# Selection matmuls for the last 16 spectrum rows, and batch 1's first stage inside the first MLP steps

## The chip, the cores and the metric

One core of a Trainium2 chip. The metric is device time of that core in microseconds (us), the median of several executions. "Step" means one of the 400 MLP steps into which the kernel's plan is cut (50 token groups of 8 steps); steps 0 to 47 belong to batch 0.

## The reference, cut to what matters

```python
# x (8, 3136, 256), filt_r and filt_i (1569, 256), U (3136, 32), V (32, 3136)
X = np.fft.rfft(x, axis=1)                       # over the 3136 tokens
y = np.fft.irfft(X * (filt_r + 1j * filt_i), n=3136, axis=1)
h = y.transpose(0, 2, 1) @ U @ V                 # low-rank token mixing
u = y + h.transpose(0, 2, 1)
out = u + np.maximum(u @ w_ch1, 0.0) @ w_ch2     # channel MLP, 256 -> 1024 -> 256
```

## The kernel before

The two transforms are matmuls over 3136 = 64 x 49, each in two stages. Stage 1 writes its result to DRAM (`ct1`) and reads it back in another order (`a`); stage 2, the filter multiply and stage 3 give the spectrum after the filter, which goes through DRAM again (`ct2`, read back as `e`); stage 4 gives `ut`, the input of the MLP. Batch 0 skips the first trip by transposing on TensorE. An eviction is the copy of a result out of TensorE's accumulators (0.59 us for 128x512 on ScalarE, line 273). Batches 1 to 7 run their stages between the MLP steps of the batch ahead, by a plan:

```python
def load_x(b, c, after=None):             # POOL issues the loads of x
    ...                                   # c == 3: the last 64 rows
        t = sb.tile([128, 4, XW], F16, tag="x", bufs=4, name="x")
        if after is not None:             # a copy that waits for `after`
            nc.gpsimd.tensor_copy(t[0:1, 0, 0:1], after[0:1, 0:1])
        for h in range(2):
            nc.gpsimd.dma_start(t[h:128:2, :, 0:2 * DM], ...)

def st1(b):                               # stage 1: 12 pieces and a last one
    for c in range(3):
        ...                               # 8 matmuls, 4 evictions into asb
        for h in range(2):                # the sync engine issues the stores
            nc.sync.dma_start(dram(ct1[b], ...), asb[64 * h:64 * h + 64])
        ...
    nc.scalar.copy(al, pf[0:64, 0:DM])    # the last piece
    nc.sync.dma_start(dram(ct1[b], ...), al)

def load_a2(b, k):                        # read-back for stage 2
    t = sb.tile([98, 4 * DM], F16, tag="a2", bufs=4, name="a2")
    nc.sync.dma_start(t, dram(ct1[b], 4 * k * DM, ...))
...
low_rank(0)
for n, _ in enumerate(st1(1)):            # stage 1 of batch 1 in the head
    ...
stage4(groups[0], 0)                      # then the first MLP step
stage4(groups[0], 1)
...
def x_after(b):                           # x of batch 2 waits for relu of step 3
    for c in range(4):
        load_x(b, c, groups[0].h[3] if c == 0 else None)
at(4, x_after, 2)
...
for n, gr in enumerate(groups):
    for t in range(8):
        ...
        mm1(gr, t)                        # first MLP matmul and relu
        if n: mm2_part(groups[n - 1], t)  # second MLP matmul of the group ahead
        for f, a in plan[8 * n + t]:      # what the plan holds for this step
            f(*a)
```

## Time and profile before

| | us |
|---|---|
| median of the runs beside the changed kernel (4) | 555.31 (554.28 to 556.38) |
| profiled run | 555.2 |
| first MLP matmul | 61.2 |
| step 48 begins (batch 0 done) | 134.7 |
| rest | 420.5 |

What the sync engine's queue issued, in order of time (start, us that the issues took, engine, line, operation, target and source, count):

```profile
49.15 0.31 SPq L329 DMA_DIRECT2D ct<-esb  x1
52.45 1.10 SPq L438 DMA_DIRECT2D e<-ct  x2
53.66 5.83 SPq L277 DMA_DIRECT2D ct<-asb  x6
59.59 1.05 SPq L286 DMA_DIRECT2D ct<-al  x1
62.65 1.62 SPq L320 DMA_DIRECT2D a<-ct  x4
```

In this program a read-back is issued only when the stores before it have landed (between 48 and 70 us the trace has the sync engine wait for `ct<-esb` ahead of its reads of `e`, 1.9 us at the longest). So the gap between a store's issue and its read's issue shows how long the store took to land, at most: 3.3 us for batch 0's last spectrum tile (49.15 to 52.45), and 3.1 us for the last piece of batch 1's stage 1 (59.59 to 62.65). Second, POOL after that:

```profile
66.50 0.18 POOL L168 COPY x<-hring 1x1 f16<-1x1 f16 x1 [12.12 <-ACT hring L492]
67.02 4.25 POOL L170 DMA_DIRECT2D x<-in_x_dram  x6 [0.33 <-POOL x L168]
```

POOL stood idle for 12.12 us until a relu of ScalarE (line 492) let it copy one element; only then did it issue the load of batch 2's x. That 1x1 copy is a hold: it keeps 1.5 MB of loads back until stage 1 of batch 1 has been stored and its read-back issued.

### The profile page before, as it was taken

To read this page: it belongs to the slowest core of one execution; us is meant where nothing else is said; L and a number is where in the kernel's file an instruction comes from. 1 tells how busy PE (TensorE), PEld (TensorE's weight loads), DVE (VectorE), ACT (ScalarE), POOL (GpSimd) and SP (SyncE) were. 2 spreads that over 40 slices of the span, in tenths; PEclk is the share of its full clock that TensorE was granted. 3 is DMA by queue.
4 is the path that set the end of the run, shared out by engine and by line. 5 is a ranking of instruction groups with operands and counts; after the bars stand their busy time and mean duration, and the time that the engine had idled before them with its cause. 6 is when DMAs were issued, how large, how long until landed. Compare 5 with 4: busy or idle time off the path is not lost.

```text
span 555.2 us, 11638 instructions
## 1 busy us (share of the span) xinstructions
PE 517.2 (93%) x4491; PEld 375.3 (68%) x4491; DVE 353.1 (64%) x409; ACT 390.8 (70%) x684; POOL 282.4 (51%) x194
## 2 busy tenths in 40 slices
PE   5976689997999999999999999999999999999996
PEld 2634356664767777777776777777786777777775
DVE  6764675755756686758846785858746887643332
ACT  8566868774777688767776788677777577765663
POOL 5778179951883165915683175806563297300000
PEclk9999899997999999999999999999999999999999
DMA  9998876894669468774879468865653553333212
GB/s 194 157 170 192 225 141 187 209 230 130 174 184 250 125 176 199 173 204 137 193 222 221 123 173 228 166 199 152 186 170 121 141 167 121 106 113 115 96 77 87
DMA packets 85432, 92.06 MB, mean 166 GB/s; under 512 B 6741, under 2 KB 69416, under 8 KB 85376
## 3 DMA queue, kind: packets, MB, share of 16 engines
q1 hardware_dynamic: 67968, 75.12, 45.5%
q0 software_dynamic: 16960, 15.91, 19.1%
q8 instruction: 35, 0.57, 0.4%
q10 hardware_dynamic: 448, 0.28, 0.3%
q14 instruction: 21, 0.17, 0.1%
HBM read 57.42 MB, written 49.77 MB: 193 GB/s over the span
## 4 chain that ended last, share of the span: by engine, by line
PE 70%; POOL 10%; DVE 7%; DMA 6%; ACT 4%; issue 2%; DVEq 0%; ACTq 0%; POOLq 0%; SPq 0%
PE psum L521 25%; PE psum L488 24%; PE psum L352 4%; PE psum L344 4%; PE psum L477 4%; PE psum L497 3%; PE psum L266 3%; POOL y L634 3%; DMA x<-in_x_dram 3%; POOL x L170 2%; DVE ut L482 1%; DVE tb L632 1%; PE psum L416 1%; DMA w1sb<-in_moe_w_ch_dram 1%; ACT asb L273 1%
## 5 line engine op out<-in xcount | busy, mean ns | idle before, releaser
L492 ACT ACTIVATE hring<-psum 128x512 f16<-128x512 f32 (+1 forms) x416 | 237.7, 576 | 104.5 <-PE psum L488 103.2
L488 PE MATMUL psum<-ut,w1sb 128*128 128x512 f16 (+1 forms) x832 | 240.3, 370 | 6.4 <-ACT hring L492 3.0
L521 PE MATMUL psum<-w2sb,hring 128*128 128x256 f16 x1536 | 230.9, 273 | 0.0
L634 POOL TENSOR_TENSOR y<-ta,tb 128x1024 f16<-128x1024 f16 x56 | 120.5, 2159 | 159.4 <-DVE tb L632 115.5
L521 PEld LDWEIGHTS <-hring 128*128 128x128 f16 x1536 | 143.3, 98 | 63.8 <-issue 3.8
L482 DVE CAST ut<-psum 128x512 f16<-128x512 f32 x96 | 71.1, 741 | 108.3 <-PE psum L477 88.2
L488 PEld LDWEIGHTS <-w1sb 128*128 128x128 f16 x832 | 104.6, 145 | 27.3 <-issue 10.4
L529 DVE COPY och<-psum 128x512 f32<-128x512 f32 x96 | 66.2, 689 | 47.3 <-PE psum L497 46.6
L326 ACT CAST esb<-psum 98x512 f16<-98x512 f32 x128 | 74.7, 586 | 21.6 <-PE psum L344 16.0
L628 DVE TENSOR_TENSOR ta<-psum,fb 128x1024 f16<-128x1024 f32 x41 | 50.0, 1218 | 7.9 <-PE psum L352 6.9
L273 ACT CAST asb<-psum 128x512 f16<-128x512 f32 x78 | 45.7, 589 | 12.3 <-PE psum L266 11.2
L497 PE MATMUL psum<-idn,ut 128*128 128x128 f16 x392 | 54.0, 220 | 0.0
L477 PEld LDWEIGHTS <-e 96*128 96x128 f16 x768 | 35.9, 99 | 25.5 <-issue 10.2
L630 DVE TENSOR_TENSOR tb<-psum,fc 64x1024 f16<-64x1024 f32 x41 | 50.3, 1226 | 0.9
L632 DVE TENSOR_TENSOR tb<-psum,fc 64x1024 f16<-64x1024 f32 x41 | 49.9, 1218 | 0.8
L477 PE MATMUL psum<-sv,e 96*128 96x64 f16 x768 | 38.8, 194 | 6.5 <-DMA e<-ct 3.7
L344 PE MATMUL psum<-y,g 128*98 128x512 f16 x105 | 39.9, 380 | 3.0 <-POOL y L634 1.5
L497 PEld LDWEIGHTS <-ut 128*128 128x128 f16 x392 | 38.4, 98 | 4.9
L628 POOL TENSOR_TENSOR ta<-pc,fb 128x1024 f16<-128x1024 f16 x15 | 32.4, 2159 | 10.7 <-ACT pc L638 10.7
L352 PE MATMUL psum<-a,w2t 98*128 98x512 f16 x113 | 34.3, 379 | 1.7 <-DVE tb L632 1.6
L266 PE MATMUL psum<-x,wf 128*128 128x256 f16 x168 | 31.3, 274 | 2.8 <-DVE asb L271 1.0
L630 POOL TENSOR_TENSOR tb<-pc,fc 64x1024 f16<-64x1024 f16 x15 | 31.8, 2122 | 1.2
(93 smaller groups left out, 373.6 us busy)
## 6 DMA issues: line engine op xcount, KB each, us to landing
out_dram<-och SPq DMA_DIRECT2D x47, 512.0 KB
ct<-esb SPq DMA_DIRECT2D x64, 196.0 KB
x<-in_x_dram POOLq DMA_DIRECT2D x48, 256.0 KB, 8.1
e<-ct SPq DMA_DIRECT2D x48, 256.0 KB
a<-ct SPq DMA_DIRECT2D x56, 196.0 KB
ct<-asb SPq DMA_DIRECT2D x42, 256.0 KB
wf<-wf SPq DMA_DIRECT2D x3, 256.0 KB
w1sb<-in_moe_w_ch_dram POOLq DMA_DIRECT2D x1, 512.0 KB, 6.8
```

Source lines behind the costliest of these rows:

```text
L326: nc.scalar.copy(esb[b, k][:, 2 * half:2 * half + 2, :].rearrange("p s d -> p (s d)"), pe[0:98])
L344: nc.tensor.matmul(pe[0:98], g3[:, m, :], v, start=(n == 0), stop=(n == len(parts) - 1))
L477: nc.tensor.matmul(pu[:, 64 * i:64 * i + 64], e2[b, c][:, i, 128 * dh:128 * dh + 128], sv[:, 64 * r:64 * r + 64], start=(i == 0), stop=Tru ...
L482: nc.vector.tensor_copy(o, v)
L488: nc.tensor.matmul(ph[:, 0:n], w1sb[:, dh, :, t], gr.ut[:, dh, 0:n], start=(dh == 0), stop=(dh == 1))
L492: nc.scalar.activation(h[:, 0:n], ph[:, 0:n], RELU)
L497: nc.tensor.matmul(o[:, dh * 128:dh * 128 + 128], gr.ut[:, dh, t0:t0 + n], idn, start=False, stop=(dh == 1), skip_group_check=True)
L521: nc.tensor.matmul(o, gr.h[tt][:, i * 128:(i + 1) * 128], w2sb[:, tt, :], start=(tt == 0), stop=False, skip_group_check=True)
L529: nc.vector.tensor_copy(gr.och[:, 2 * y:2 * y + 2, :].rearrange("p j d -> p (j d)"), gr.pc)
L628: eng.tensor_mul(ta, p, va)
L630: eng.tensor_mul(tb[0:64], p[64:128], vb[64:128])
L634: nc.gpsimd.tensor_add(ys[k], ta, tb)
```

## The change

Its intent is to shorten the head, the time before the first MLP step. Four parts matter here:

1. The first token group of batch 0 needs all 64 spectrum rows. 48 are read back from DRAM early; the last 16 are picked out of on-chip tiles by matmuls with 0/1 matrices (`sel`), and the low-rank term H gets its own matmul into the same accumulator.
2. VectorE does all 16 spectrum multiplies of batch 0 (POOL did four).
3. Ten of the thirteen pieces of batch 1's stage 1 go from the head into MLP steps 0 to 4; six of that batch's eight spectrum tiles take a form with twice the TensorE work and less filter preparation.
4. Loads move: w1 behind a copy of V on POOL, w2 behind the first `ut`, and x of batch 2 to steps 4 to 7.

The diff, cut to its core (the whole also halves the stage-1 table's load and trims tiles to 113 partitions):

```diff
 def mid_first():
+        def pick(j):                     # rows 48..63 by selection
+            for i in range(2):
+                sl = 2 * (j - 12) + i
+                for g in range(4):
+                    nc.tensor.matmul(zp[32 * g:32 * g + 32], sel[:, g, 28 - 4 * sl:60 - 4 * sl],
+                                     esb[0, j // 2][:, 2 * (j % 2) + i, :], ...)
 ...
+                if k == 5:
+                    load_e2(0, 0, 48)    # the 48 rows of the first group
 ...
         for c in range(4):
             load_x(1, c)
-        nc.gpsimd.dma_start(w2sb, moe_w_ch2.rearrange("(cc t) e -> cc (t e)", t=8))
+        nc.gpsimd.tensor_copy(sv[64:96, :]..., vnat...)
+        nc.gpsimd.dma_start(w1sb, moe_w_ch1...)
 ...
-            if j in (7, 9, 12, 14): ...  # POOL multiply
+            nc.vector.tensor_mul(uv, pz[0:NZ], fin)
 ...
-    for n, _ in enumerate(st1(1)): ...
+    for k in (4, 5, 0, 1, 2, 3):
+        make_fc(k, nc.gpsimd.tensor_copy)
+    nc.gpsimd.tensor_copy(w2sb[0:1, 0, DM:DM + 1], groups[0].ut[0:1, 0, 0:1])
+    nc.gpsimd.dma_start(w2sb[:, :, 0:DM], ...)
 ...
+            for k, q in ((4, 5), (0, 5), (1, 5), (5, 6), (2, 12), (3, 15), (6, 18), (7, 22)):
+                at(q, fetch, k)          # read-backs of batch 1 at steps 5 ..
+            for k, q, d in ((4, 9, 18), (5, 17, 27)):
+                at(q, two, k)            # first stage 2 at step 9
 ...
-    at(4, x_after, 2)
+    for n in range(5):
+        for _ in range(2):
+            at(n, step1, 1)              # stage 1 of batch 1
+    for c in range(4):
+        at((4, 4, 6, 7)[c], load_x, 2, c)
+        at((33, 38, 43, 45)[c], load_x, 3, c)
 ...
-            plan_st1(b, 12, (0, 1, 3, 4, 5, 7))
+            plan_st1(b, 16, (0, 1, 3, 4, 5, 7))     # b == 2
```

## The prediction

> **What bounds the kernel now.** I read the page's slices first, then busy time in stretches that I chose, then the chain that ended last over the first 62 us, then TensorE in order of time where it is not full. One slice is 555.2/40 = 13.9 us:
>
> ```profile
> PE   5976689997999999999999999999999999999996
> ...
> PEclk9999899997999999999999999999999999999999
> DMA  9998876894669468774879468865653553333212
> ```
>
> TensorE is full from the sixth slice on, with one dent (slice 10, 125 to 139 us, where the clock falls too) and a short tail. So from there only removed TensorE work helps; before it, and in the dent, what helps is an earlier end of a wait. The stretches give sizes (61.2 us is the first MLP matmul, line 488; counting its pairs in order of time, the 48 MLP steps of batch 0's six groups end at 134.68 us):
>
> ```profile
> core 0: us, PE busy (x) PEld busy (x) DVE busy (x) ACT busy (x) POOL busy (x), PEclk, DMA share, GB/s
> 0.00:61.20 61.20, 44.95 (x312) 26.55 (x313) 36.77 (x45) 41.14 (x47) 39.91 (x50) 0.94 0.99 186
> ...
> 61.20:134.68 73.48, 60.69 (x503) 42.27 (x500) 50.03 (x61) 50.50 (x87) 47.28 (x33) 0.96 0.77 181
> 134.68:555.20 420.52, 411.55 (x3684) 306.51 (x3682) 266.27 (x304) 299.12 (x550) 195.23 (x111) 1.00 0.58 160
> ```
>
> Three terms, then: a head of 61.2 us, batch 0's MLP of 73.5 us in which TensorE is idle 73.48 - 60.69 = 12.8 us, and a rest of 420.5 us that is TensorE-bound (411.55 busy). The head's chain ends so:
>
> ```profile
> 45.26 2.13 POOL uv L397
> ...
> 48.69 1.08 PE psum L416 x32
> ...
> 53.82 0.88 PE psum L266 x6
> ...
> 57.03 2.72 PE psum L234 x6
> ...
> 60.21 0.74 DVE ut L482
> ```
>
> The last of 16 spectrum multiplies waits for POOL (2.13 us against 1.17 to 1.22 us on VectorE). Then come the low-rank product, stage 1 of batch 1 (line 266, 50.2 to 56.6), warming matmuls (line 234), and the first group's stage 4, which also needs the spectrum written to DRAM and read back. From the last spectrum row (about 48.6) to the first MLP matmul are 12.6 us. The dent:
>
> ```profile
> 125.76 0.61 PE L488 MATMUL psum<-ut,w1sb 128*128 128x512 f16 x2
> 130.09 0.58 PE L477 MATMUL psum<-sv,e 96*128 96x64 f16 x8 [3.73 <-DMA e<-ct]
> ...
> 131.32 1.06 PE L488 MATMUL psum<-ut,w1sb 128*128 128x512 f16 x2
> ```
>
> Batch 1's spectrum came back from DRAM too late by 3.7 us, and the same pair of matmuls afterwards takes 1.06 instead of 0.61 us.
>
> [...] the idle 3.73 us are followed by 1.04 to 1.06 us pairs until 135.5, so the dent costs more than its wait. [...] 32 low-rank matmuls of 256 columns span 1.08 us, some 34 ns each, against 109 ns start to start for the full-width ones (four of line 521 begin in about 0.437 us). The new selection matmuls have that form. [...]
>
> **The change, part by part.** *Start.* The table for stage 1 is loaded at half size and doubled by two VectorE scalings; U comes as float32. About 0.2 MB less precedes x, at some 190 GB/s 1 us. x bounds this part (the chain shows it from 5.05 to 19.07 us), so I give 1 us: the first spectrum multiply at about 24 instead of 25.1.
>
> *Middle.* All 16 multiplies go to VectorE. The first seven before take 25.1 to 33.8, 1.24 us each with their gaps, since ScalarE has its turn-back copies (1.01) and evictions (0.58) beside them. 16 x 1.24 = 19.8, so the last ends near 44; before, POOL's last ended at 47.4.
>
> *First group.* Its first 48 rows come by DRAM while the rest computes; the last 16 are picked by matmul from the evicted tiles. After the multiply: stage 3 about 0.8, eviction 0.6, the last picks and low-rank matmuls 0.5, copies of both results 0.4, the H matmul and its copy 0.3 + 0.4, the last matmul 0.3, the two halves of ut at once on VectorE and ScalarE 0.75, and about eight handovers of some 0.05 to 0.1: 4.7 us, so 48.7. Two waits can exceed it: the 48 rows are stored near 40.5, and before it took 3.3 us from the last eviction to the read's issue and some 3 us to land, so about 47 against the 45.5 at which TensorE asks; and w1 now follows POOL's 6.95 us copy of V (about 33 to 40), so it lands near 40.5 + 6.8 = 47.3. I add 1.5 us: first MLP matmul at **50**, 11 us earlier.
>
> *Batch 0's MLP.* TensorE is busy 60.7 us there before, some 3.5 of it the slow clock after the dent: 57.2 of work. Added: ten of the thirteen pieces of batch 1's stage 1, nine pairs x 0.218 + 0.1 = 2.1 us. Six of the eight spectrum tiles of batch 1 take the two-product form, which doubles stages 2 and 3: per tile 8 matmuls of 512 columns instead of 4, 6 x 4 x 0.217 = 5.2 us. Together 64.5. Removed from this stretch: the three 1.89 us filter copies on ScalarE that held up relu (63.6 to 68.2) and 8.7 us of idle time mostly in the first nine steps; and the dent, as batch 1's spectrum is now planned to be whole by step 31 of 48. Added idle: with no mm2 yet, steps 0 to 7 are paced by relu at 0.58 plus stage 1's evictions, 1.5 us; w2 is asked for at step 8 (about 57.5) but issued only after ut at about 51, and before it took 13.6 us (7 for w1), so 2 us; other small waits 1.5. That makes 64.5 + 5 = **69.5** instead of 73.5.
>
> *Rest.* Same groups, same matmuls, same lead of the later batches: 420.5. 113 partitions instead of 128 do not shorten a row.
>
> Sum: 50 + 69.5 + 420.5 = **540.0 us**, 15.3 less.
>
> **Rivals.** (a) *A new wait at steps 8 to 9.* w2 (a 0.5 KB-piece transfer gated by ut), batch 1's first stage-2 inputs (written after step 4, read back at step 5, wanted at step 9), and x for batch 2 all fall on the DMA between 51 and 65 us. For it: the 13.6 us landing of w2 and the head's full DMA. Against: these waits overlap, and x is not needed until step 16. It would cost 4 us plus about as much slow clock: 547. (b) *POOL becomes the bound in the head or in batch 0.* It gets the V copy before w1, six filter copies before w2 and eight more later; [...] If w2 waits for six of the slow ones, it is issued at 54.5: 545. Before, POOL is busy 47 of 73 us in this stretch and gives up one tile of three, so later it should hold. (c) *All waits vanish:* 48.7 + 66 + 420.5 = 535. (d) *The head is transfer-bound anyway,* as its 0.99 share suggests: less is moved ahead of the first MLP step (w2 of 1 MB is put off), against it; if true, only 5 us are won: 548 to 550.
>
> **Range and chances.** (c) is the low side, (a) and (b) the high side: 533 to 548. "Faster by over 2%" means below 544.2; it needs 11.1 of the expected 15.3 us. A single one of (a) or (b) at its full size would lose that, and I give them together with (d) about one in five. Slower needs a stall of over 26 us: a mis-ordered queue only.
>
> **What would show it.** Right: the first line-488-type matmul near 50; no POOL multiply in the head and VectorE multiplies back to back at about 1.2 us; TensorE busy near 64 us in the following 69; no wait for a DMA of e near step 46 and full clock there; the last 344 steps still 420 us. Wrong: a wait for w2, a or w1 of over 3 us with a clock dent between 48 and 65 us; a first MLP matmul after 54; or a rest that differs by more than 3 us, which would mean that an engine beside TensorE, not shown full today, was tipped over.

What no trace of this case shows is cut from the recorded text, as marked: three rules of the hardware, and the price of a POOL copy in rival (b). No term of the sum is cut: it came to 50 + 69.5 + 420.5 = 540.0 us, as recorded. The "slow ones" of rival (b) are copies at the 2.2 ns an element of V's copy (6.95 us for 3136 elements, line 562), by estimate 2.3 us for 1024. Where the text gives no figure, the trace of the kernel before has these: the granted clock was 0.5 for 3.4 us from 40.0 and again from 57.0, and for 6.8 us from 128.7 (half of that, 3.4 us, is what the text has as 3.5 of slow clock after the dent); the handovers read off were 0.04 to 0.08 us (POOL's multiply ended at 47.38 and its matmul began at 47.42; ScalarE's copy ended at 45.18 and POOL began at 45.26); and VectorE's multiply of 1024 elements took 1.23 us on 64 partitions (line 630) and 1.22 on 128 (line 628).

## The result, and the profile after

The changed kernel took 578.19 us (577.65 to 578.78, 4 runs) against 555.31: ratio 1.0412, 95% interval 1.039 to 1.0434. It is slower by 4.1%, where 540.0 was predicted. All outputs are right. Ratios here are the mean time of one kernel's fast runs over that of the other's of the same rounds, so not quite the ratio of the medians quoted.

The slices of the changed kernel (14.4 us each; PEclk is the granted TensorE clock, in tenths of full speed):

```profile
PE   5885638896899999999999999999999999999997
...
PEclk9995859998999999999999999999999999999999
DMA  9994963478567946886587656795655444343212
```

The page before had one dent after the head, in slice 10. Here TensorE dips at the end of the head (slices 4 to 5) and again in slices 6 and 10, the first two with a clear fall of the clock (to 0.5 in slices 4 and 6, 0.8 in slice 10). By stretches, cut at the first MLP matmul and at the end of batch 0's steps:

```profile
core 0: us, PE busy (x) PEld busy (x) DVE busy (x) ACT busy (x) POOL busy (x), PEclk, DMA share, GB/s
0.00:55.06 55.06, 38.39 (x320) 20.90 (x321) 37.32 (x47) 26.14 (x39) 37.11 (x50) 0.90 0.93 175
55.06:154.90 99.84, 73.89 (x541) 48.20 (x541) 49.34 (x62) 49.20 (x88) 40.45 (x38) 0.87 0.67 150
154.90:575.80 420.90, 411.68 (x3685) 306.40 (x3683) 266.60 (x304) 299.24 (x550) 195.17 (x111) 1.00 0.59 160
```

The rest is as predicted (420.9 against 420.5). The head missed by 5.1 us (55.1 against 50) and batch 0's MLP by 30.3 (99.8 against 69.5): its TensorE idle time is 99.84 - 73.89 = 26.0 us, where 12.8 stood before and 5 was expected. What TensorE waited for between 40 and 160 us (line, waited for: us in all, times, longest):

```profile
PE psum L385 <- DMA a<-ct: 18.4, 2, 14.0
PE psum L486 <- DMA ct<-esb: 7.5, 1, 7.5
```

And in order of time:

```profile
49.00 1.03 PE L486 MATMUL psum<-sv,e 48*128 48x64 f16 x16 [7.50 <-DMA ct<-esb]
55.06 1.02 PE L588 MATMUL psum<-ut,w1sb 128*128 128x512 f16 x2 [0.39 <-DVE ut L506]
...
80.78 1.01 PE L385 MATMUL psum<-a,w2t 98*128 98x512 f16 x2 [13.97 <-DMA a<-ct]
```

Three waits, each for a round trip through DRAM. TensorE stood 7.5 us for the first group's 48 rows (41.5 to 49.0), 13.97 us for batch 1's first read-back (66.8 to 80.8), and 4.4 us for batch 2's (136.1 to 140.5). The label in the first line names a store; the data wanted is the read that waits for it. The sync engine's queue shows each trip:

```profile
37.46 0.31 SPq L362 DMA_DIRECT2D ct<-esb  x1
...
45.93 0.32 SPq L537 DMA_DIRECT2D e<-ct  x1
...
57.62 10.29 SPq L299 DMA_DIRECT2D ct<-asb  x6
68.01 3.17 SPq L308 DMA_DIRECT2D ct<-al  x1
77.83 1.63 SPq L348 DMA_DIRECT2D a<-ct  x4
...
131.48 0.85 SPq L308 DMA_DIRECT2D ct<-al  x1
...
137.69 1.19 SPq L348 DMA_DIRECT2D a<-ct  x3
```

Store to read's issue: 8.5 us in the head (3.3 before), 9.8 us for batch 1 (3.1 before), 6.2 us for batch 2. In the second trip the row of the six stores spans 10.29 us instead of 5.83. Part of that is waiting for pieces of stage 1, which now come out of MLP steps 0 to 4: taken one by one, the six issues last 6.56 us, 4.85 before. The difference is nearly all in the sixth, 2.92 us against 1.03 before:

```profile
64.99 2.92 SPq L299 DMA_DIRECT2D ct<-asb  x1
```

The small store after it took 3.17 us to issue, 1.05 before. What POOL issued beside it:

```profile
58.64 3.69 POOL L187 DMA_DIRECT2D x<-in_x_dram  x6
```

The six large loads of batch 2's x went out from 58.64, in the middle of the stores (57.62 to 71.2), where before they began at 67.02, after the read-back's issue. The plan put them into steps 4 to 7. But nothing made these loads wait for their steps: POOL issued them as it came to them, from 58.64 on, while step 4 began at 61.65.

Counting the DMA packets that the trace shows per microsecond shows what became of the stores. (A packet of the trace is one piece of 512 bytes, 1 KB or more; a few of 4 bytes are counted too.) The left number is POOL's queue (loads, with w2), the right one the sync engine's (512-byte stores):

```
us from     before: 56    57    58    59    60    61
POOL | sync       0|541 0|648 0|608 0|471 0|467 0|475
us from     after:  57    58    59    60      61
                  98|0  347|0 373|0 217|263 14|629      (w2's packets)
us from     after:  66      67      68      69      70      71      72      73      74     75
                  134|82  149|137 147|146 145|152 149|145 148|148 148|152 111|384 41|531 10|218   (x's 1 KB packets)
```

Between 67 and 72 us each queue gets about 148 packets a microsecond, where the stores alone had 467 to 648. x's pieces took 97 ns each in that time and the stores' 39 (30 for stores alone). At 148 a microsecond against the 535 that the first row averages, the stores went at little over a quarter of their rate. The counts were not always equal: from 63 to 65 us x had 144 and 176 packets a microsecond and the stores 0 and 1, though the second pair of stores had been issued at 60.86 to 62.21 (in the kernel before, the first packet of these stores came 2.0 us after the issue, 53.66 to 55.62). The stores of stage 1 are 6 x 512 + 64 = 3136 packets; alone, at 535 a microsecond, they need 5.9 us, beside x at 148 they would need 21 (estimates from these rates).

### The profile page after: what moved, and what is told of

Its sections match the earlier page's. It is cut to its first block, busy times and chain, and to the rows that moved or that the text cites. A ratio compares the mean times of both kernels' runs of the same rounds, so it can differ in the third digit from the quotient of the medians.

```text
span 575.8 us, 11739 instructions
## 1 busy us (share of the span) xinstructions
PE 524.0 (91%) x4543; PEld 375.5 (65%) x4543; DVE 353.3 (61%) x411; ACT 374.6 (65%) x676; POOL 272.7 (47%) x199
## 4 chain that ended last, share of the span: by engine, by line
PE 62%; POOL 5%; DVE 3%; ACT 2%; issue 1%; ACTq 0%; POOLq 0%; DVEq 0%
PE psum L621 23%; PE psum L588 23%; PE psum L385 3%; PE psum L377 3%; PE psum L597 3%; PE psum L577 3%; PE psum L291 2%; POOL y L722 2%; DVE tb L720 1%; PE psum L515 1%; POOL x L187 1%; POOL tb L720 1%; POOL ta L716 1%; POOL tb L718 1%; DVE ut L582 1%
## 5 line engine op out<-in xcount | busy, mean ns | idle before, releaser
L722 POOL TENSOR_TENSOR y<-ta,tb 113x1024 f16<-113x1024 f16 x50 | 107.8, 2161 | 161.9 <-DVE tb L720 146.4
L582 DVE CAST ut<-psum 128x512 f16<-128x512 f32 x94 | 69.8, 742 | 119.3 <-PE psum L577 102.4
L385 PE MATMUL psum<-a,w2t 98*128 98x512 f16 x124 | 38.2, 386 | 23.7 <-DMA a<-ct 18.4
L716 DVE TENSOR_TENSOR ta<-psum,fb 113x1024 f16<-113x1024 f32 x36 | 43.9, 1219 | 12.4 <-PE psum L385 6.2
L716 POOL TENSOR_TENSOR ta<-pc,fb 113x1024 f16<-113x1024 f16 x14 | 30.2, 2156 | 37.7 <-ACT pc L726 37.7
L718 DVE TENSOR_TENSOR tb<-psum,fc 49x1024 f16<-49x1024 f32 x36 | 44.1, 1226 | 0.9
L720 DVE TENSOR_TENSOR tb<-psum,fc 49x1024 f16<-49x1024 f32 x36 | 43.9, 1218 | 1.0
L577 PE MATMUL psum<-sv,e 96*128 96x64 f16 x752 | 37.6, 193 | 2.1 <-ACT asb L295 1.5
L377 PE MATMUL psum<-y,g 113*98 113x512 f16 x94 | 35.9, 382 | 2.1 <-ACT esb L355 1.1
L291 PE MATMUL psum<-x,wf 128*128 128x256 f16 x168 | 34.1, 289 | 2.2 <-DVE ut L582 1.8
L385 PEld LDWEIGHTS <-w2t 98*128 98x128 f16 x146 | 13.2, 98 | 31.2 <-issue 26.3
```

Of the source, the lines that this page charges most:

```text
L385: nc.tensor.matmul(pz, w, a, start=True, stop=True)
L577: nc.tensor.matmul(pu[:, 64 * i:64 * i + 64], e2[b, c][:, i, 128 * dh:128 * dh + 128], sv[:, 64 * r:64 * r + 64], start=(i == 0), stop=Tru ...
L582: (nc.scalar.copy if gr is groups[0] and dh else nc.vector.tensor_copy)(o, v)
L716: eng.tensor_mul(ta, p[0:NZ], va)
L720: eng.tensor_mul(tb[64:NZ], p[0:NR], vb[0:NR])
L722: nc.gpsimd.tensor_add(ys[k], ta, tb)
```

## The experiments

Eighteen kernels ran, 3 or 5 rounds each. Edits are against the changed kernel unless said. All results in one table; "head" is the first MLP matmul, "a1" and "a2" the longest wait for batch 1's and batch 2's read-back, "step 48" the start of batch 1's MLP, all us of the profiled run ("none": under 1 us); the before column is the median of the same job. The jobs ran on different chips, so compare ratios rather than medians across jobs.

| kernel | median | before | ratio (95%) | head | a1 | a2 | step 48 |
|---|---|---|---|---|---|---|---|
| changed | 578.19 | 555.31 | 1.0412 (1.039 to 1.0434) | 55.1 | 13.97 | 4.38 | 154.9 |
| gate_x2 | 573.49 | 557.31 | 1.0271 (1.022 to 1.0322) | 56.5 | 8.82 | 5.14 | 151.7 |
| w2_plain | 577.96 | 557.31 | 1.0357 (1.0307 to 1.0408) | 55.3 | 13.37 | 4.47 | 153.6 |
| x1_late | 578.33 | 557.31 | 1.0364 (1.0318 to 1.0411) | 51.5 | 12.41 | 4.19 | 154.6 |
| before_x2_free | 563.73 | 557.31 | 1.0110 (1.0057 to 1.0162) | 58.2 | 9.54 | none | 139.9 |
| gate_a2 | 576.63 | 555.76 | 1.0354 (1.0288 to 1.0421) | 56.3 | 4.69 | 4.64 | 153.6 |
| mid2_late | 578.81 | 555.76 | 1.0390 (1.0324 to 1.0456) | 56.0 | 14.87 | 3.77 | 155.4 |
| st1_head | 574.65 | 555.76 | 1.0320 (1.0253 to 1.0387) | 55.0 | 11.32 | 4.21 | 150.5 |
| three | 574.59 | 555.76 | 1.0312 (1.0226 to 1.0398) | 55.6 | 3.58 | 4.04 | 151.6 |
| x2_twice | 586.38 | 558.57 | 1.0502 (1.0441 to 1.0562) | 55.9 | 21.88 | 4.70 | 163.4 |
| warm | 577.12 | 558.57 | 1.0333 (1.0263 to 1.0403) | 54.5 | filled | 4.51 | 152.3 |
| four | 566.68 | 558.57 | 1.0129 (1.0071 to 1.0187) | 55.7 | 7.57 | 1.59 | 142.9 |
| w1_after | 576.68 | 556.54 | 1.0354 (1.0297 to 1.0412) | 54.0 | 12.10 | 5.01 | 152.8 |
| x3_late | 579.52 | 556.54 | 1.0407 (1.0349 to 1.0466) | 56.7 | 14.39 | 4.53 | 156.4 |
| five | 558.96 | 556.54 | 1.0041 (0.9962 to 1.012) | 55.8 | none | 1.05 | 134.7 |
| six | 564.45 | 556.54 | 1.0137 (1.0081 to 1.0193) | 57.0 | none | 1.15 | 139.6 |
| x3_held | 573.22 | 558.45 | 1.0295 (1.0235 to 1.0354) | 54.7 | 13.72 | 1.54 | 148.7 |
| seven | 558.97 | 558.45 | 1.0030 (0.9981 to 1.0079) | 54.4 | none | 2.92 | 137.2 |
| eight | 556.64 | 557.41 | 0.9991 (0.9951 to 1.0032) | 56.0 | none | 1.67 | 132.5 |

**Theory:** x of batch 2, sent without its hold, slows stage 1's stores; that makes the 14 us wait. **Rivals:** w2's 512-byte pieces do it; the order of the stages (stage 1 moved into the MLP) does it; or the fall of the clock to 0.5 costs most of it.

### Holding x back, and its reverse on the kernel before

gate_x2 holds x of batch 2 until relu of step 8; gate_a2 holds it until the third read-back of batch 1 has landed; before_x2_free takes the hold out of the kernel before.

```diff
-        at((4, 4, 6, 7)[c], load_x, 2, c)
+    def x2():
+        for c in range(4):
+            load_x(2, c, groups[1].h[0] if c == 0 else None)   # gate_a2: a2s[1, 1]
+    at(8, x2)
# before_x2_free, on the kernel before:
-            load_x(b, c, groups[0].h[3] if c == 0 else None)
+            load_x(b, c, None)
```

> The changed kernel, with the four loads of x for batch 2 held back until relu of step 8 has written (one POOL copy of one element, as the kernel before had it on an earlier relu). Theory A (the x loads of batch 2, issued at 58.6 to 62.9 us, crowd out the stage-1 stores of batch 1 and so delay their read-back): the 13.97 us wait for a at step 9 falls to about 3 us or less, half of the slow clock after it goes, and the time falls by 11 to 15 us to 563 to 567. Theory B (stage 1 of batch 1 inside the MLP steps is simply done too late for its DRAM round trip): the wait stays above 8 us and the time above 571. Theory C (the load of w2 is what crowds): the wait stays above 10 us, the time above 575.

> The kernel before, with the hold on the x loads of batch 2 taken away, so that POOL issues them right after its copy of V at 54.4 us, while the stage-1 stores of batch 1 are on their way. Theory A: the read-back of a comes late by 5 to 10 us, TensorE waits for it in the first MLP steps, and the time rises by 5 to 12 us to 560 to 567. If the crowding is peculiar to the changed kernel: 553 to 557.

> The changed kernel, with the x loads of batch 2 held back until the third of the read-backs a of batch 1 has landed (the hold at step 8's relu was still too early: the loads went out at 67.9 us, the read-back at 69.8, and that took 7 us to land). Theory A: the read-back lands about 3.5 us after its issue, the wait for a (13.97 us in the changed kernel, 8.82 with the earlier hold) falls to some 5 us, and the time to 568 to 571. If the rest of the wait is theory B alone (stage 1 ends too late): no better than the earlier hold, 573.

With gate_x2 the wait fell from 13.97 to 8.82 us and the row of the stores to 7.3 us (the sixth store took 0.69 us to issue, not 2.92):

```profile
59.08 7.30 SPq L299 DMA_DIRECT2D ct<-asb  x6
66.48 0.91 SPq L308 DMA_DIRECT2D ct<-al  x1
69.82 1.85 SPq L348 DMA_DIRECT2D a<-ct  x4
```

The last store now lands in 3.3 us. Without its hold the kernel before got a wait of 9.54 us where it had 0.68 (the row of its six stores spans 11.02 us instead of 5.83, and from 59 to 66 us both queues had 134 to 155 packets a microsecond), and became 1.1% slower, though its first MLP matmul came 3.0 us earlier. So the hold is worth 1.1 to 1.4% here, and its removal makes the wait. With gate_a2 the wait is 4.69 us, yet the time is hardly better: a new wait of 5.85 us appears behind it, at a stage 2 whose accumulators were still held by an earlier multiply. That multiply, on VectorE, had waited for POOL:

```profile
88.40 1.23 DVE L747 TENSOR_TENSOR uv<-psum,fb 113x1024 f16<-113x1024 f32 x1 [6.09 <-POOL y L724]
```

POOL's held x issue (74.90 to 79.6) stands ahead of its own spectrum multiplies in its queue. The hold stops an engine that also computes (the 6.09 us of this line).

The 4.69 us that stay with x out of the way are, read from the trace, stage 1's place in the MLP steps: its last store goes out only at 65.80 and the read at 69.18, while TensorE wants `a` at 67.4. So x made some 9 of the 14 us.

### Doubling the suspect

x2_twice sends six more loads of the same size as x's into a spare tile, just ahead of the real ones.

```diff
+    def x_again():
+        for c in range(3):
+            for h in range(2):
+                nc.gpsimd.dma_start(cm[h:128:2, 2048 * c:2048 * c + 2048]..., dram(x.tensor, ...))
+    at(4, x_again)
```

> The changed kernel, with the six large x loads of batch 2 sent twice, the first time into a tile that nothing reads any more. Theory A in its sharper form ([...] in the changed kernel some 150 of 512 B a microsecond on each, against some 530 on the stores' queue alone): the stores are held up by about as much again, the 13.97 us wait for a grows by 8 to 14 us, the time to 586 to 593. If the x loads are not what holds the stores up: within 3 us of 578.

The wait grew to 21.88 us, by 7.9. The sixth store took 7.69 us to issue (1.03 in the kernel before, 2.92 in the changed kernel), the small one after it 3.12. An estimate from the packet rates: 1536 more packets of 1 KB at 148 a microsecond last 10.4 us, in which as many stores pass that alone would have taken 1536 / 535 = 2.9 us, so +7.5. Dose and response fit: held longer 4.69, held 8.82, free 13.97, doubled 21.88.

### w2's form

w2_plain loads w2 in whole rows instead of 512-byte pieces.

```diff
-    nc.gpsimd.dma_start(w2sb[:, :, 0:DM], moe_w_ch2.rearrange("(cc t) e -> cc t e", t=8))
+    nc.gpsimd.dma_start(w2sb, moe_w_ch2.rearrange("(cc t) e -> cc (t e)", t=8))
```

> The changed kernel, with w2 in its old layout (no padding, so 4 KB pieces for 0.5 KB ones), still issued after the first ut. Theory C (w2's small pieces crowd the queue between 55 and 62 us): the wait for a at step 9 shrinks by over 4 us, time below 573. Theory A: nothing beyond noise, 576.5 to 579.

13.37 us instead of 13.97, and the same time within the noise. The form of w2's load is not the cause. No run took w2's load alone away. Beside it the stores' first packet came 2.6 us after the issue (3.1 in w2_plain), 2.0 in the kernel before. But with x held the last store lands in 3.4 us (gate_a2) and 3.3 (gate_x2), w2's packets being through by 63.

### Where stage 1 stands

st1_head puts all 13 pieces of batch 1's stage 1 back ahead of the first MLP step; mid2_late starts batch 2's spectrum work three steps later; three joins both with gate_a2.

```diff
# st1_head
-        step1(1)                    # and the two below it, and those of steps 0 to 4
+        for _ in range(13):
+            step1(1)
# mid2_late
-        m = later(start[b - 1], (16, -9, -12)[min(b, 3) - 1])
+        m = later(start[b - 1], (16, -6, -12)[min(b, 3) - 1])
```

> The changed kernel, with all 13 pieces of stage 1 of batch 1 done while TensorE waits for the first group's read-back (41.5 to 49 us), none in the MLP steps. Theory B (part of the wait at step 9 is that stage 1 was put into the MLP steps): the pieces are hidden in the head's wait, the first MLP matmul stays at 54 to 56 us, the wait for a at step 9 falls from 14 to under 5 us, time 563 to 568. Theory A alone (only the x loads matter; they still go out at 58 to 63 us): the wait stays at 9 us or more, time above 571.

> The changed kernel, with the spectrum work of batch 2 begun 6 steps ahead of its batch instead of 9. Theory: the third wait (4.38 us for a of batch 2, 1.77 us and 6.8 us of half clock after it) comes from stage 1 of batch 2 being moved from steps 12 on to steps 16 on, while its reader stayed: with the reader 3 steps later it goes, and the time falls by 6 to 9 us to 569 to 572. Rival (the reader's wait is only moved, since the later groups need the result at the same time): within 2 us of 578.

> The three above together: x of batch 2 held back until a of batch 1 has landed, batch 2's spectrum work 3 steps later, stage 1 of batch 1 in the head's wait. If the three waits are separate, first MLP matmul at about 55 us, 48 steps in 70 to 74 us, the rest 420 us: 546 to 551 us, faster than both kernels. If one only hides behind another: 555 to 562.

Stage 1 in the head leaves 11.32 us of the wait: by itself the place of the matmuls moves only 2.65 us (and about 0.9% of the time), as x still goes out beside the stores. mid2_late moved 0.6 us of the third wait, and another for VectorE's `ut` grew from 1.8 to 2.6: no gain. three brings the wait for `a` to 3.58 but puts 6.71 us in its place, the same queueing behind POOL as in gate_a2. In three the last store still took 6.8 us to its read's issue (60.16 to 66.92), beside w2's packets (205|195 from 60 us): with x gone and stage 1 early, w2's load has a part too.

### The head's wait

x1_late sends x of batch 1, except its first part, after the first group's 48 rows have landed; w1_after does that with w1.

```diff
# x1_late
                 if k == 5:
                     load_e2(0, 0, 48)
+                    for c in range(1, 4):
+                        load_x(1, c, e2[0, 0][0:1, 0] if c == 1 else None)
# w1_after
+    nc.gpsimd.tensor_copy(w1sb[0:1, 0, 0, 0:1], e2[0, 0][0:1, 0, 0:1])
+    nc.gpsimd.dma_start(w1sb, moe_w_ch1.rearrange("(h dd) c -> dd h c", h=2))
```

> The changed kernel, with three of the four loads of x for batch 1 held back until the read-back of the first 48 spectrum rows has landed. Theory A at the head (x of batch 1 crowds out the store of spectrum tile 5, which took 8.1 us from issue to landing): the 7.5 us wait for e falls below 3 us, the first MLP matmul comes at 49 to 51.5 us instead of 55.1, without half clock; the total falls by 3 to 7 us only, as the second wait stays. Rival (store and read-back take this long by themselves, some 11 us): the first MLP matmul stays after 54 us and the total within 2 us of 578.

> The changed kernel, with w1 sent only after the read-back of the first 48 spectrum rows has landed (before: at 36.6 us, just ahead of the store of spectrum tile 5 at 37.5). Theory: w1's 2 KB packets are the half of the head's wait that holding x of batch 1 back did not remove; the store lands some 3 us sooner, the wait of 7.5 us falls to 4 to 5; but w1 then lands at 50 to 52, so the first MLP matmul comes at 51 to 54. Total 574 to 579, as the second wait stays. If w1 has no part in it: the wait stays above 7 us and the first MLP matmul comes later, at 56 to 58.

The wait of 7.5 us fell to 4.13 without x and to 5.58 without w1; each takes part, neither alone. x1_late starts the MLP 3.6 us earlier (51.5). But POOL, behind its held loads, then comes late to its filter copies and to w2's load: TensorE waits 2.6 us for w2, and 2.7 us for an eviction on VectorE, whose two filter scalings took 2.33 us beside POOL's copies instead of 0.76. The time is unchanged. w1_after starts it at 54.0, since the first MLP matmul now waits 1.2 us, by its place for w1 itself (the trace's label names a filter scaling). In x1_late's trace the stores got no packet at all for 3 us while w1's 2 KB packets flowed (from 38, 39, 40 us: 13|0, 99|0, 107|0), then 48|358. The store stood issued from 37.44 and got its first packet at 41.32; beyond the 2.0 us to a first packet in the kernel before, some 1.9 us are left, in which the counts were not equal as from 67 to 72 us in the changed kernel; why stays open.

### The clock

warm fills the first two waits with matmuls whose result nobody reads (34 and 60 of 512 columns).

```diff
+        for _ in range(34):
+            nc.tensor.matmul(pu[0], cm[:, 6784:6912], cm[:, 6272:6784], start=True, stop=True)
...
+            at(9, warm, 60)
```

> The changed kernel with useless matmuls in its first two waits: 34 ahead of the first group's read-back (7.4 us at full clock against a wait of 7.5), 60 ahead of batch 1's first spectrum tile (13 us against 13.97). They measure what the half clock after a wait costs by itself. Theory: 17.1 + 13.7 us at half rate vanish, of which TensorE is busy in some 14; half of that, less what relu and evictions pace, is won: 4 to 7 us, time 571 to 574, with no less DMA. If the half clock costs nothing of its own: 577 to 581.

The mean clock rose from 0.967 to 0.994, but the median fell by only 1.1 us (the ratios differ by 0.8%, their intervals overlap, and step 48 came 2.6 us earlier). The stretches of the changed kernel at a granted clock of 0.5 (from 43.6 for 17.1 us, from 70.9 for 13.7, from 139.2 for 6.8; the pair of 512-column matmuls at 55.06 took 1.02 us, at full clock 0.60) come to 37.6 us, of which 16.6 lie inside the three waits and 11.7 between the first and the second. The author's reading of the small gain, that work done faster ahead of a transfer only lengthens the wait for it, was not shown. So the clock is a companion of the waits with 1 to 4 us of its own; a closer figure stays open.

### The third wait

x3_late only moves batch 3's loads in the plan. x3_held puts a hold on the second of them.

```diff
# x3_late
-        at((33, 38, 43, 45)[c], load_x, 3, c)
+        at((33, 41, 45, 47)[c], load_x, 3, c)
# x3_held: the same, but
+    at(41, lambda: load_x(3, 1, groups[5].h[1]))
```

> The changed kernel, with x loads two to four of batch 3 at steps 41, 45 and 47 instead of 38, 43 and 45. Theory: the load at step 38 (packets from 130 to 135 us) meets the last stage-1 stores of batch 2 (issued 129.9 to 131.5, landed 137.7); without it they land some 3 us sooner, the third wait falls from 4.38 to about 1 us, time 573 to 576. If the third wait has another cause: 577 to 580.

> The changed kernel, with the second x load of batch 3 held until relu of step 41 has written (some 144 us). Theory: the last stage-1 stores of batch 2 then land some 3 us sooner and the third wait falls from 4.4 to 1 to 2 us; time 573 to 576. If the wait stays at 4 us or more, these stores and their read-back take that long by themselves and the cause is that stage 1 of batch 2 was put 4 steps later: 577 to 580.

x3_late tested nothing: POOL issued that load at 130.58 us all the same, and the wait stayed at 4.53. Moving a line in the plan moves only its place in POOL's queue. With the hold the read-back goes out 3.7 us after the last store (6.2 in the changed kernel):

```profile
130.47 2.10 SPq L308 DMA_DIRECT2D ct<-al  x1
134.19 1.19 SPq L348 DMA_DIRECT2D a<-ct  x3
```

The wait fell from 4.38 to 1.54 and the time to 573.22 us, 5 us less (ratio 1.0295 against 1.0412). It is the same effect one batch later: stores that land later beside loads of x.

### Taking all the waits away

four joins st1_head, mid2_late, read-backs at steps 1 and 2, w2 without its gate, x of batch 2 held by relu of step 4 and x3_late's steps. five also takes three reads of later groups out of the sync engine's way. six adds w1_after, seven adds 24 filling matmuls to five, eight adds x3_held's hold to seven.

```diff
# four, beside st1_head and mid2_late
-    nc.gpsimd.tensor_copy(w2sb[0:1, 0, DM:DM + 1], groups[0].ut[0:1, 0, 0:1])
-            for k, q in ((4, 5), (0, 5), (1, 5), (5, 6), ...
+            for k, q in ((4, 1), (0, 1), (1, 1), (5, 2), ...
+            load_x(2, c, groups[0].h[4] if c == 0 else None)      # at step 4
# five, on four
-                if k == 7:
-                    load_e2(0, 1, 64, 48)
-                    load_e2(0, 2)
-                    load_e2(0, 6)
...                                      # the same three lines, behind the 13 step1(1)
# seven, on five
-        for _ in range(13):
-            step1(1)
+        for n in range(24):
+            if n < 13:
+                step1(1)
+            nc.tensor.matmul(pu[0], cm[:, 6784:6912], cm[:, 6272:6784], start=True, stop=True)
# eight, on seven
+    at(41, lambda: load_x(3, 1, groups[5].h[1]))
-        m = later(start[b - 1], (16, -6, -12)[min(b, 3) - 1])
+        m = later(start[b - 1], (16, -9, -12)[min(b, 3) - 1])
```

> The changed kernel with its transfers in another order: stage 1 of batch 1 in the head's wait; w2 sent when POOL is free (about 43 us, while the DMA is near idle) and not after ut; a of batch 1 read back from step 1 on; x of batch 2 after relu of step 4, so behind those reads in time and ahead of POOL's multiplies; the second x load of batch 3 at step 41 instead of 38, and batch 2's spectrum work 3 steps later. If the waits of the changed kernel all come from stores and read-backs meeting POOL's loads: first MLP matmul at 54 to 56 us, no wait over 3 us after it, step 48 at 124 to 130, total 546 to 553 us, faster than the kernel before. If a wait remains or is only moved: 558 to 570.

> The run 'four' with one thing changed: the three reads of spectrum rows that wait for the last spectrum store to land now stand behind batch 1's stage-1 stores in the sync engine's order, so that those stores go out at about 48.7 instead of 54.1 us. Theory: a of batch 1 then lands 4 to 5 us sooner, the 7.57 us wait of 'four' falls below 3 us, time 559 to 563 (four: 566.7). If the sync engine's order does not matter: 565 to 568.

> The run 'five' with w1 sent only after the first read-back, as in w1_after. If both gains hold: first MLP matmul at 51 to 54 us, time 555 to 560, about the kernel before. If w1 and w2 now only meet the stage-1 stores of batch 1 instead (they share the microseconds from 46 to 58): 562 to 570, worse than 'five'.

> The run 'five' with 24 useless 512-column matmuls among the pieces of stage 1 of batch 1, so that TensorE's clock does not fall at 45 us. If the half clock is what stretches the chain from the read-back to the first MLP matmul (5.1 us in five): that matmul comes at 53 to 54.5 instead of 55.8, time 556 to 558 where five had 559, equal to or just below the kernel before. If the chain is set by copies and handovers: no change beyond 0.5 us.

> The run 'seven' with the remedy of x3_held for the third wait: the second x load of batch 3 really held until step 41, and batch 2's spectrum work begun 9 steps ahead again. If both waits at the end of batch 0 shrink as in x3_held (to about 1.5 and 1.8 us, from 2.9 and 1.9 in the trace of seven): 1 to 3 us less than seven, so 0.99 to 1.00 of the kernel before. If not: as seven, 1.00 to 1.005.

four still waited 7.57 us: the sync engine issued the first stage-1 store only at 54.11, since the three reads stood ahead of it and waited for batch 0's last spectrum tile to land. In five the stores go out at 48.66, the read-back is issued 7.6 us earlier than in four (58.43 against 66.02) and 16 earlier than in st1_head (74.45), and 0.7 us of wait for it is left:

```profile
48.66 6.25 SPq L299 DMA_DIRECT2D ct<-asb  x6
55.01 1.03 SPq L308 DMA_DIRECT2D ct<-al  x1
...
58.43 1.73 SPq L348 DMA_DIRECT2D a<-ct  x4
```

five took 558.96 us, 7.7 less than four (ratio 1.0041 against 1.0129). six lost 5.5 of that again: its first MLP matmul waited 2.1 us for w1, its clock in batch 0 was 0.93 against 0.95, and idle time was 13.2 instead of 11.2 us. seven's first MLP matmul came 1.4 us earlier than five's (54.4), but its ratio of 1.0030 is that of five within the noise: the filling won nothing that shows. eight is the best:

```profile
core 0: us, PE busy (x) PEld busy (x) DVE busy (x) ACT busy (x) POOL busy (x), PEclk, DMA share, GB/s
0.00:56.00 56.00, 46.14 (x362) 25.19 (x363) 42.16 (x54) 27.76 (x42) 37.74 (x51) 0.97 1.04 196
56.00:132.50 76.50, 64.58 (x523) 44.25 (x523) 45.42 (x55) 47.10 (x85) 40.00 (x38) 1.00 0.76 178
```

556.64 us against 557.41 (ratio 0.9991): equal to the kernel before, not better. No version beat both kernels.

## Why the prediction was wrong

**Right.** The rest of the run (420.9 against 420.5) and with it the claim that no engine beside TensorE was tipped over there. All multiplies on VectorE at about 1.2 us, with none on POOL. The multiplies even came earlier than 24 to 44 us:

```profile
20.84 2.36 DVE L475 TENSOR_TENSOR uv<-psum,fb 113x1024 f16<-113x1024 f32 x2 [0.74 <-ACT a L341]
...
29.93 10.27 DVE L475 TENSOR_TENSOR uv<-psum,fb 113x1024 f16<-113x1024 f32 x9 [0.35 <-PE psum L385]
```

They span 20.8 to 40.2. Rival (b), POOL as the bound through slow copies, fell: its six filter copies took 5.95 us in all, some 1.0 each (0.97 ns an element of a partition, against 2.2 for the strided copy of V, 6.97 us for 32x3136), and w2 was issued at 55.45 just after `ut`. The 2 us priced for w2 did not come: TensorE first used it at 65.23 without a wait.

**Nearly right.** The TensorE work in batch 0's stretch. Eight, at full clock, has 64.58 us there without the stage-1 pieces; with the 2.1 us predicted for these, 66.7 against 64.5. The rest of the 73.89 us busy in the changed kernel is slower clock, about 7 us. An estimate from the stretches at clock 0.5, half of the time outside the waits: 2.8 us before the second wait, 1.9 after it, 2.7 after the third. One reading of the trace was off, without weight in the sum: of the three filter copies on ScalarE, two lie between 63.6 and 68.2.

**Wrong: the head's read-back.** The step read "before it took 3.3 us from the last eviction to the read's issue and some 3 us to land". That was measured on a queue that had only those stores (49.15 to 52.45 before). In the changed kernel x of batch 1 and w1 are in flight at the moment of the store, and it took 8.5 + 3.1 us (37.46, 45.93, 49.00). TensorE asked at 41.5, earlier than assumed, and got the data at 49.0 instead of 47. x1_late and w1_after show that both loads take part. This step and the 6.1 us from there to the first MLP matmul (at a granted clock of 0.50) make 55.1 instead of 50.

**Wrong: "Added idle", 5 us, and the size of rival (a).** This is the step that decided. Rival (a) named the place, "A new wait at steps 8 to 9", and the three transfers, but gave it 4 us and as much slow clock. Its argument against was "these waits overlap, and x is not needed until step 16", and the 5 us have no term for the read-back of `a`. The transfers did meet where it said ("between 51 and 65 us"), but they did not overlap for free: the trip from store to read's issue grew from 3.1 to 9.8 us, TensorE waited 13.97 us, and idle time was 26.0 us. What counted here was not when x is needed but when it was sent. The diff removed the argument `groups[0].h[3]`, and the prediction does not mention that a hold went with it: POOL issued x of batch 2 at 58.64, some 8 us earlier than the kernel before did, into the stores of stage 1. Shown by: the wait grows and shrinks with x's sending (gate_x2, gate_a2, x2_twice), and the kernel before gets it too (before_x2_free). x is some 9 of the 14 us; the rest is stage 1's place (4.69 us in gate_a2) and went only when stage 1, the read-backs and the order of the sync engine's queue changed together (five). Two of the prediction's own signs of being wrong came: a first MLP matmul after 54, and a wait for `a` of over 3 us, though later (66.8) than its 48 to 65. A second case of the same, batch 3's x beside batch 2's stores, was not foreseen at all (4.4 us; x3_held).

**Wrong: the dent "as batch 1's spectrum is now planned to be whole by step 31 of 48".** The old dent did go, and another stands in its place, from batch 2's read-back.

**Where the gain went in the end.** With these waits gone (eight), the head is 5.2 us shorter than before, and batch 0's stretch 3.0 us longer (76.5 against 73.48), though at full clock and without the old dent. Its TensorE work is larger by the two-product form (5.2 us predicted), and its idle time is 11.9 instead of 12.8 us, not 5: small waits for VectorE (4.2 us in five of them behind the multiplies, 1.8 for `ut`), where the sum had 1.5 us for "other small waits". That leaves 553.0 us in the profile against 555.2, which the timed runs do not tell from zero. Against the 540 predicted, the best version still lacks 6 us in the head and 7 us of idle time in batch 0.

**Open.** The clock's own cost (1 to 4 us); how the head's 7.5 us splits between x and w1, as their effects overlap; w2's part in the second wait; and the stretches in which a queue with work got no packets.

## What to carry to other kernels

A transfer's price was not its own here (beside x's loads the stores fell from 535 packets a microsecond to 148): ask of each load that moves at which moment it is *sent*, what releases it, and which stores or read-backs are in flight then; a small copy that makes an engine wait may be there only to hold a load back (without the 1x1 copy the kernel before was 1.1% slower). A position in a plan is not a time for an engine that runs ahead of it (x's loads went out from 58.64, their first step began at 61.65). A latency measured in a quiet place of the trace must not be reused for a busy one (3.3 us became 8.5), and a hold on an engine that also computes stops its work too (the 5.85 us in gate_a2; a hold on another engine was not tried).
